# Transposing the last token tiles and the blocks' tokens on TensorE instead of by DMA

## The chip, the cores and the metric

The program runs on one core of a Trainium2 chip. A core has TensorE (PE in the profile; PEld is its weight load), VectorE (DVE), ScalarE (ACT), GpSimd (POOL) and SyncE (SP); SP and POOL issue the transfers here, SP ordinary ones and DMA transposes, POOL the ones that gather or scatter rows by a table of row numbers. Each engine works through its own instructions in the order in which they were emitted and waits on semaphores for the others. The metric is the device time in microseconds of one execution.

## The reference

Three layers follow one another on 1536 tokens of 512 numbers:

```
x = attention(q, k, v)            # only pairs whose 6 hash bits agree; 2 x 8 heads of 768 x 64
out = sum over e of P[:, e] * (relu(x @ w1[e]) @ w2[e])     # first mixture: 8 experts, 1024 hidden units
idx = argmax(normalised(x) @ normalised(emb).T / tau)       # second mixture: each token goes to one expert
out[mask_e] = gate * (relu(x[mask_e] @ w1b[e]) @ w2b[e])    # mask_e: the tokens with idx == e
```

The kernel keeps numbers as two float16 parts, a high and a low one, and forms a product from three matmuls (high x high, high x low, low x high).

## The kernel before

**Up to the last expert.** Attention, and the first mixture with each expert's first product in Winograd's form, fill the first 1167 us or so. They are not touched.

**The last products of the first mixture.** The tokens are twelve tiles of 128, numbered 0 to 11 in the order in which they are finished. Tiles 8 to 11 come last, in `mm2s(E - 1, 2, last_tile)` (line 1569): 24 matmuls of 512 columns for each tile (line 932). When a tile's sum is complete, `finish_tile` (line 1059) adds it to `acc` on VectorE (L1425), writes its high part on ScalarE (L195) and its low part on VectorE (L196) into rows `xf`, has SP transpose these rows into `xt` by DMA (L1067), and has SP write the rows to memory (L1069) for later gathers.

**The router.** For each tile `route_logits` (12 tiny matmuls, L1078, tile `rl`, which read `xt`; then five small VectorE steps, L1081 to L1085) picks the tokens' experts, and `route_rank` (two tiny matmuls, L1089 and L1090, then VectorE) counts each token's place within its expert. After tile 11 `place` sorts the remaining tokens into blocks of at most 128 tokens of one expert: a long chain of small VectorE steps (L1138 to L1108), 12 tiny matmuls (`pid`, L1171), then the blocks' row numbers (L1175), the six first gathers of tokens, and the gates (L1022 to L1317 on VectorE, then 24 tiny matmuls `pg`, L1323).

**The blocks of the second mixture.** 22 slots are laid out, of which four can be filled from the first eight tiles alone, before the last tiles are known; in the profiled execution 17 blocks ran (0 to 16). A block j takes its tokens' rows by a gather on POOL (`gather_x`, L1362), which SP transposes by DMA (L1364), and its weights by two gathers on POOL (`gather_w`, L1345), unless they are there already. `block1(j)` is 96 matmuls of 128 columns (L1381) in two halves, each followed by ScalarE (L1386) and VectorE (L1387); `block2(j)` is 24 matmuls of 512 columns (L1398), then VectorE scales (L1407) and POOL scatters the result (L1412).

**What sets the order.** From line 1515 on an agenda does: `paced(gen, per)` counts a step after every `per` matmuls it emits, and `at(d, f)` puts `f` d steps later. A step is 4 matmuls in the last products (six steps for a tile), 32 in `block1` and 8 in `block2` (six steps for a block). `DT = (20, 15, 10, 6)` steps after tiles 8, 9, 10 and 11 come their logits, `DR` steps after that the rank. Since TensorE works in emission order, a tiny matmul that waits for a transfer holds all matmuls behind it.

Of the kernel before, what the change touches and what calls it, by code (L numbers as in the profile page):

```python
# [10 lines left out]
F16 = mybir.dt.float16  # L11
# [22 lines left out]
# columns of the constant table: they follow from the shapes alone  # L34
# [56 lines left out]
class Plan:  # L91
    """Puts tasks in the order in which the engines would come to them: each engine takes the task of lowest
    rank whose inputs are there and whose buffers are free. Tasks are then emitted in that order."""
# [58 lines left out]
def tile_kernel(ctx, tc, q, k, v, proj, wg, w1, w2, emb, tau, w1b, w2b, cst, out):  # L152
# [76 lines left out]
    def plan_pair(p):  # L229
# [6 lines left out]
        # load  # L236
# [11 lines left out]
        def qk(w):  # L248
# [28 lines left out]
            if not first:  # L277
                a = add(("hi", p, w), he, hu, hi(slice(0, 2)), after=[L[w]], rank=rk, take=take)
                a = add(("lo", p, w), DVE, 0.98, lo(slice(0, 2)), after=[a], rank=rk)
            else:  # L280
                # the first head waits for nothing else: its way to the tensor engine is the shortest
                h0 = add(("hi0", w), ACT, 0.4, hi(0), after=[L[w]], rank=-90, take=take, order=[T.get(("hi0", 0))])
                l0 = add(("lo0", w), DVE, 0.46, lo(0), after=[h0], rank=-90)
                t0 = add(("pt", w), PE, 0.65, tr0, after=[l0, T["ident"]], rank=-90, take=("st",))
                cb = add(("cb", w), ACT, 0.75, lambda: nc.scalar.activation(out=Bt[i][:, 0], in_=q_.t[w], func=AF.Copy), after=[t0], rank=-85)
                add(("ca", w), DVE, 0.87, lambda: nc.vector.tensor_copy(out=At[i][0:64, 0], in_=q_.t[w][r:r + 64]), after=[t0], order=[cb], rank=-85, give=("st",))

                def bits0(m):
                    q_.__dict__.setdefault("pb", {})[w] = mx_tile(m)
                    for g in range(2):  # L290
                        for n in range(3):
                            nc.tensor.matmul(out=q_.pb[w][64:96, g, 0:384], lhsT=Wp[w][n], rhs=Bt[i][:, 0, g * 384:(g + 1) * 384], start=(n == 0), stop=(n == 2))

                def thr0():
                    s1, s2 = (cc["thr"], cc["msc"]) if w == 0 else (cc["thrk"], cc["msck"])
                    nc.vector.tensor_scalar(out=At[i][64:88, 0].rearrange("p (g s) -> p g s", g=2), in0=q_.pb[w][64:88, :, 0:384],
                                            scalar1=s1[64:88], scalar2=s2[64:88], op0=ALU.is_gt, op1=ALU.mult)

                bd = add(("bd", w), PE, 1.5, bits0, after=[cb, T["pj2"]], rank=-84, take=(MX,))
                add(("bt", w), DVE, 0.87, thr0, after=[bd], rank=-84, give=(bd,))  # L300
                a = add(("hi", p, w), ACT, 0.4, hi(1), after=[L[w]], order=[h0, T.get(("hi0", 0))], rank=-80)
                a = add(("lo", p, w), DVE, 0.46, lo(1), after=[a], rank=-80)
# [14 lines left out]
        # bits of the hash  # L317
# [26 lines left out]
        # sums of the values  # L344
# [19 lines left out]
        # the pair's columns of x, in two parts, transposed  # L364
# [23 lines left out]
    def plan_head(p, a, q_, C, V, SV):  # L388
# [44 lines left out]
        # the first head's halves follow one another; the others have their maxima in time  # L433
# [11 lines left out]
        for g in range(2):  # L445
# [3 lines left out]
            for c0 in range(0, NC, 2):  # L449
# [17 lines left out]
                def l(eng, g_=g_, c0=c0):  # L467
                    # the upper halves of float32 are bfloat16 values: the first part; the second is what they leave
# [44 lines left out]
    def w_piece(dst, src, j, m):  # L513
        """rows j*m*128.. of src [rows, n] into dst[:, j*m:(j+1)*m, 2, n]"""
        n = src.shape[1]
        t = sgp.tile([P, m, n], F32, tag="sg", name="sg")
        nc.sync.dma_start(out=t, in_=src[j * m * P:(j + 1) * m * P].rearrange("(c p) f -> p c f", p=P))
        return t
# [26 lines left out]
    def mm1(pool, ps_tile, e, t0, n):  # L545
        """hidden units of tokens t0..t0+n"""
# [22 lines left out]
    with tc.manual_schedule():  # L569
# [19 lines left out]
        def pj_parts():  # L589
            # the projection in three parts whose products with the parts of q and k are exact  # L590
# [35 lines left out]
        # the accumulators of the filling products take the place of one of the tiles for the maximum  # L626
# [9 lines left out]
        def fill():  # L636
            """the first expert on the first half of the tokens, in pieces that fill the tensor engine's pauses"""
# [91 lines left out]
        # the parts of the tokens' sums (see mm1s), and the weights' parts: five pieces that take turns  # L729
# [5 lines left out]
        # scratch: the second mixture's weights in two parts, a row for each expert and partition  # L735
# [42 lines left out]
        def w1_jobs(e, p):  # L778
            """columns p and p + 4 of W1 (in chunks of 128), quarters a11 and a12 above a21 and a22 (columns by rows),
            and the sums of quarters; parts of a11, a12, a22, s2, s3, s4, s1"""  # L780
# [32 lines left out]
        # every split is preceded by its load, sgp_bufs pieces ahead  # L813
# [23 lines left out]
        def unit_x(k, l, u, h):  # L837
            """a half of a unit's tokens: a half's tokens meet tokens of the same sequence in the other half"""
# [4 lines left out]
        def token_sums(u):  # L843
            """B12 - B11 (T1), B22 - B12 (T3), B21 - T2 (T4) and B22 - T1 (T2) of the quarters B of x (halves of its
            columns by halves of the unit's tokens)"""
# [26 lines left out]
        def mm1s(e, u):  # L872
            """hidden units of a unit, two tiles in each half: of the quarters of W1 and x, seven products instead
            of eight (Winograd's form of Strassen's algorithm)"""
# [144 lines left out]
        def newton_sqrt(n, p, out, sq, tmp):  # L1019
            """out = sqrt(sq), the table's value refined once"""  # L1020
# [38 lines left out]
        def finish_tile(o):  # L1059
            """a token tile's mixture is complete: keep it in two parts, and choose its expert"""  # L1060
# [6 lines left out]
            nc.sync.dma_start_transpose(out=xt, in_=xf)  # L1067
# [4 lines left out]
            return xt  # L1072
# [25 lines left out]
        def rank_parts(t0, t1):  # L1098
            """the full blocks before each rank and its place in its block"""
# [35 lines left out]
        def count_blocks(limits, op):  # L1135
            """how many of the limits each expert's tokens reach; the sums up to each expert"""
# [4 lines left out]
        def order_blocks():  # L1141
            """experts with more blocks come first; the blocks before each expert's and up to them"""
# [7 lines left out]
        def slot_experts(j0, j1, blocks):  # L1150
            """the expert of each slot's block; expert 0 without a block"""
# [21 lines left out]
        def slot_reads(ps, j0, j1):  # L1173
            """an empty place reads row 0 and writes nowhere"""
# [7 lines left out]
        def early_place():  # L1182
            """The first tiles hold at least one full block of an expert's tokens, whatever the choices: the first
            such blocks are the first slots. A slot that gets none stays empty."""
# [19 lines left out]
        def early_rest_of_loads():  # L1204
            """what needs the space of the last products' operands"""
# [42 lines left out]
        def place():  # L1248
            """the other blocks, of at most 128 tokens of one expert"""
# [10 lines left out]
            # a third of the blocks for each weight buffer, its blocks in that order  # L1260
# [7 lines left out]
        def late_experts(jb, ld):  # L1268
            """a slot's weights are fetched unless their buffer holds them already"""
# [60 lines left out]
        BW = {}  # L1330
        xbT = {}
# [23 lines left out]
        def gather_x(j):  # L1355
# [8 lines left out]
            turn = lambda: nc.sync.dma_start_transpose(out=xbT[j], in_=xb)  # L1364
            if j == 3:
                at(X3T, turn)
            else:
                turn()
# [40 lines left out]
        def scatter(n):  # L1409
            """the first of the outputs that are ready go to their rows"""  # L1410
# [21 lines left out]
        def route_step():  # L1432
            """moves the tiles that are complete through the router, a stage at a time"""
# [10 lines left out]
        def run(gen, per, jobs=None, n=1):  # L1444
            """emits a unit's matmuls; after every `per` of them a piece of other engines' work, `jobs` in `n` pieces"""
# [11 lines left out]
        def start_expert(e):  # L1457
            """the work beside this expert's products: the next expert's weights, the second mixture's weights"""
# [3 lines left out]
            def spread(heavy, light, n=1, m=0):  # L1462
                """the second half of a piece comes after n light ones"""
# [67 lines left out]
        def last_tile(t, ps):  # L1531
            mix(E - 1)(t, ps)
            at(DT[t - TE], route_logits, t, pending.pop()[1])
# [42 lines left out]
        at(W3T, third_weights)  # L1576
        for j in range(2):
            paced(block1(j), 32)
            paced(block2(j), 8)
# [5 lines left out]
        # each slot that may stay empty has its condition; the last ones, which hardly any choice of experts needs, share one  # L1585
        c = ExitStack()
        for j in range(2, NBLK):
# [7 lines left out]
            if EARLY < j and j + XAHEAD - 1 < NBLK:  # L1595
                gather_x(j + XAHEAD - 1)
            paced(block2(j), 8)
# [7 lines left out]
DT = (20, 15, 10, 6)  # L1605
DR = (2, 2, 2, 2)
# [12 lines left out]
X3T = 12  # L1619
# [37 lines left out]
```

## Time and profile before

| | us |
|---|---|
| median of 3 runs | 1446.8 |
| lowest and highest | 1440.62, 1452.34 |
| profiled execution, first to last instruction (span) | 1424.0 |
| TensorE busy, in the profiled execution | 1338.6 (94%) |
| VectorE, ScalarE, GpSimd busy | 842.0, 529.7, 507.2 |

Of the profiled execution only the span is given; it is 22.8 us under the median of the three runs, which also hold what lies around the instructions. The stretch that the change touches is the last sixth, from about 1167 us on. Times in a row are from the span's start. A bracket at a row's end is the idle time of its engine just ahead of it, and what ended it; "issue" means that nothing in the trace held the engine.

### The profile page before, as it was taken

To read this page: it belongs to the slowest core of one execution; us is meant where nothing else is said; L and a number is where in the kernel's file an instruction comes from. 1 tells how busy PE (TensorE), PEld (TensorE's weight loads), DVE (VectorE), ACT (ScalarE), POOL (GpSimd) and SP (SyncE) were. 2 spreads that over 40 slices of the span, in tenths; PEclk is the share of its full clock that TensorE was granted. 3 is DMA by queue.
4 is the path that set the end of the run, shared out by engine and by line. 5 is a ranking of instruction groups with operands and counts; after the bars stand their busy time and mean duration, and the time that the engine had idled before them with its cause. 6 is when DMAs were issued, how large, how long until landed. Compare 5 with 4: busy or idle time off the path is not lost.

```text
span 1424.0 us, 28018 instructions
## 1 busy us (share of the span) xinstructions
PE 1338.6 (94%) x11536; PEld 888.9 (62%) x11536; DVE 842.0 (59%) x1590; ACT 529.7 (37%) x799; POOL 507.2 (36%) x406
## 2 busy tenths in 40 slices
PE   5888999989999999999999999999999997699996
PEld 3565666545666666666666666666666664466664
DVE  8999764158576765765775676576665573421111
ACT  3576544233444444434443443343343331001110
POOL 4667746042465421431431342142141122123321
PEclk9999999999999999999999999999999999899998
DMA  5664401212145426434332443643511249498595
GB/s 156 155 193 124 102 18 13 56 60 105 45 134 177 133 74 207 134 104 154 99 111 103 135 127 104 207 134 104 193 44 45 68 137 299 143 315 306 187 320 139
DMA packets 152813, 194.61 MB, mean 137 GB/s; under 512 B 79246, under 2 KB 114910, under 8 KB 149864
## 3 DMA queue, kind: packets, MB, share of 16 engines
q1 hardware_dynamic: 146392, 137.70, 33.1%
q0 software_dynamic: 6288, 55.06, 10.9%
q8 instruction: 93, 1.52, 0.4%
q14 instruction: 40, 0.33, 0.1%
HBM read 128.76 MB, written 43.25 MB: 121 GB/s over the span
## 4 chain that ended last, share of the span: by engine, by line
PE 75%; DVE 11%; DMA 4%; issue 3%; POOL 3%; SPq 2%; ACT 1%; another core or an unknown queue 0%; DVEq 0%; POOLq 0%; ACTq 0%
PE h L932 28%; PE h L887 25%; PE h L1381 4%; PE y L1398 4%; DVE m L404 3%; PE st L457 2%; DMA w1m<-W1S,widx 2%; PE av L479 2%; PE hy L688 2%; PE hy L658 2%; PE h L552 1%; PE h L564 1%; POOL tc L853 1%; DMA tq<-tq 1%; SPq L1364 1%
## 5 line engine op out<-in xcount | busy, mean ns | idle before, releaser
L932 PE MATMUL h<-w,ht 128*128 128x512 f16 x2016 | 439.6, 379 | 0.0
L932 PEld LDWEIGHTS <-ht 128*128 128x128 f16 x2016 | 196.4, 98 | 231.8 <-POOL ht L903 0.3
L903 POOL TENSOR_TENSOR ht<-C,ht 128x1024 f16<-128x1024 f32 x63 | 134.2, 2130 | 522.9 <-ACT C L902 520.3
L894 DVE TENSOR_TENSOR C<-h,C 128x256 f32<-128x256 f32 x588 | 230.6, 420 | 129.4 <-PE h L887 118.2
L887 PEld LDWEIGHTS <-wm 128*128 128x128 f16 x2268 | 221.4, 98 | 31.7 <-issue 3.7
L472 POOL TENSOR_TENSOR el<-e 128x768 f16<-128x768 f32 x85 | 132.8, 1568 | 87.0 <-ACT e L460 86.4
L887 PE MATMUL h<-Tq,wm 128*128 128x256 f16 x1296 | 159.5, 273 | 0.9 <-DVE Tq L862 0.9
L887 PEld LDWEIGHTS <-wx 128*128 128x128 f16 x1260 | 122.9, 98 | 15.7
L887 PE MATMUL h<-xT,wm 128*128 128x256 f16 x972 | 127.7, 273 | 2.2 <-DVE acc L1425 1.1
L917 ACT ACTIVATE C<-h 128x256 f32<-128x256 f32 x84 | 32.1, 382 | 232.1 <-PE h L887 139.7
L196 DVE SCALAR_TENSOR_TENSOR pre<-sg,pre 128x1024 f16<-128x1024 f32 x64 | 86.3, 1356 | 51.6 <-ACT pre L195 51.6
L460 ACT ACTIVATE e<-st 128x384 f32<-128x384 f32 x192 | 86.5, 489 | 64.5 <-PE st L457 61.3
L898 ACT ACTIVATE ht<-C 128x1024 f16<-128x1024 f32 x84 | 88.3, 1051 | 39.8 <-DVE C L894 39.7
L195 ACT ACTIVATE pre<-sg 128x1024 f16<-128x1024 f32 x64 | 66.7, 1051 | 93.6 <-DMA W1S<-pre 33.7
L1398 PE MATMUL y<-bw,hx 128*128 128x512 f16 x408 | 96.5, 393 | 0.3 <-ACT hx L1386 0.2
L1425 DVE SCALAR_TENSOR_TENSOR acc<-h,Pm,acc 128x512 f32<-128x512 f32 x84 | 62.6, 745 | 53.2 <-PE h L932 52.5
L1386 ACT ACTIVATE hx<-h 128x512 f16<-128x512 f32 x34 | 20.3, 597 | 186.0 <-PE h L1381 122.3
L887 PE MATMUL h<-Tq,wx 128*128 128x256 f16 x720 | 88.7, 273 | 0.0
L804 POOL TENSOR_TENSOR tq<-sw 128x256 f32<-128x256 f32 x56 | 52.3, 935 | 74.7 <-PE hy L688 31.1
L1387 DVE SCALAR_TENSOR_TENSOR hx<-h,hx 128x512 f16<-128x512 f32 x34 | 23.5, 691 | 89.4 <-ACT hx L1386 82.7
L479 PEld LDWEIGHTS <-e 128*128 128x128 bf16 x1152 | 64.1, 98 | 13.1 <-issue 1.9
L887 PE MATMUL h<-xT,wx 128*128 128x256 f16 x540 | 72.2, 273 | 0.0
(300 smaller groups left out, 1982.0 us busy)
## 6 DMA issues: line engine op xcount, KB each, us to landing
sg<-in_moe_w_dram SPq DMA_DIRECT2D x100, 512.0 KB
W1S<-pre SPq DMA_DIRECT2D x32, 512.0 KB
W2S<-pre SPq DMA_DIRECT2D x32, 512.0 KB
sw<-in_moe_w_dram SPq DMA_DIRECT2D x56, 256.0 KB
ld<-in_q_dram SPq DMA_DIRECT2D x8, 384.0 KB
ld<-in_k_dram SPq DMA_DIRECT2D x8, 384.0 KB
ld<-in_v_dram SPq DMA_DIRECT2D x8, 384.0 KB
X2D<-xx SPq DMA_DIRECT2D x8, 256.0 KB
```

What stands on the lines that cost most here:

```text
L195: nc.scalar.activation(out=hi, in_=src, func=AF.Copy, scale=scale)
L196: nc.vector.scalar_tensor_tensor(out=lo, in0=src, scalar=scale, in1=hi, op0=ALU.mult, op1=ALU.subtract)
L460: nc.scalar.activation(out=g_.e[c0][:, c % 2, :], in_=g_.st.pop(c), func=AF.Exp, scale=2.0 ** -11)
L472: (nc.gpsimd if eng == POOL else nc.vector).tensor_tensor(out=g_.el[c0], in0=e, in1=hi, op=ALU.subtract)
L479: mm = lambda out, l, r, start=False, stop=False: nc.tensor.matmul(out=out, lhsT=l, rhs=r, start=start, stop=stop, skip_group_check=True)
L887: nc.tensor.matmul(out=ps[:, 0:UT], lhsT=w[:, i, c * P:(c + 1) * P], rhs=b(kc, j), start=(m == 0), stop=(m == len(seq) - 1))
L894: nc.vector.tensor_tensor(out=o, in0=ps[:, 0:UT], in1=x, op=ALU.add)
L898: nc.scalar.activation(out=hi, in_=C, func=AF.Relu)
L903: nc.gpsimd.tensor_tensor(out=lo, in0=C, in1=hi, op=ALU.subtract)
L932: nc.tensor.matmul(out=ps, lhsT=ht[:, a, p, h, i * P:(i + 1) * P], rhs=W2[e][:, h * 4 + p, b, :], start=(m == 0), stop=(m == len(seq) - 1))
L1398: nc.tensor.matmul(out=y, lhsT=h[:, fc, a, :], rhs=w[:, fc, b, :], start=(m == 0), stop=(m == len(seq) - 1))
L1425: nc.vector.scalar_tensor_tensor(out=acc[:, t, :], in0=ps, scalar=Pm[:, t, e:e + 1], in1=acc[:, t, :], op0=ALU.mult, op1=ALU.add)
```

## The change

- The DMA transposes of tiles 8 to 11 and of all blocks' rows go (tiles 0 to 7 keep theirs).
- A new function `turn` does each on TensorE: eight transposes of 128 x 128 into a PSUM tile `tn`, and one VectorE copy of 128 x 1024 to `xt`.
- Tiles 8 to 11 are turned `TT` = 4, 4, 4, 2 steps after they are finished; their logits come after `DT` = 7, 7, 6, 3 steps in place of 20, 15, 10, 6, their ranks after 2, 2, 1, 1 more in place of 2, 2, 2, 2. So `place` comes four steps earlier in the emission order.
- Block 0's rows are turned just ahead of its first product, those of block j + 1 between the two products of block j.

```diff
         split(xf[:, 0:DM], xf[:, DM:], acc[:, t, :], 512.0)
         nc.scalar.activation(out=jk, in_=acc[:, t, :], func=AF.Square, accum_out=ss[:, o, :])
-            nc.sync.dma_start_transpose(out=xt, in_=xf)
+            if o < TE:
+                nc.sync.dma_start_transpose(out=xt, in_=xf)
...
-            return xt
+            return xt if o < TE else (xt, xf)
+
+        def turn(xt, xf):
+            ps = ps_.h.tile([P, 2 * KC, P], F16, tag="h", name="tn")
+            for c in range(2 * KC):
+                nc.tensor.transpose(out=ps[:, c, :], in_=xf[:, c * P:(c + 1) * P], identity=ident)
+            nc.vector.tensor_copy(out=xt, in_=ps)
...
-            turn = lambda: nc.sync.dma_start_transpose(out=xbT[j], in_=xb)
-            if j == 3:
-                at(X3T, turn)
+            if j < TURN:
+                xrow[j] = xb
             else:
-                turn()
+                nc.sync.dma_start_transpose(out=xbT[j], in_=xb)
+
+        def turn_x(j):
+            if j < min(TURN, NBLK):
+                turn(xbT[j], xrow.pop(j))
...
             mix(E - 1)(t, ps)
-            at(DT[t - TE], route_logits, t, pending.pop()[1])
+            xt, xf = pending.pop()[1]
+            at(TT[t - TE], turn, xt, xf)
+            at(DT[t - TE], route_logits, t, xt)
             at(DT[t - TE] + DR[t - TE], ranked, t)
...
+        turn_x(0)
         for j in range(2):
             paced(block1(j), 32)
+            turn_x(j + 1)
             paced(block2(j), 8)
...
             paced(block1(j), 32)
             if EARLY < j and j + XAHEAD - 1 < NBLK:
                 gather_x(j + XAHEAD - 1)
+            turn_x(j + 1)
             paced(block2(j), 8)
...
-DT = (20, 15, 10, 6)
-DR = (2, 2, 2, 2)
+TURN = 99
+TT = (4, 4, 4, 2)
+DT = (7, 7, 6, 3)
+DR = (2, 2, 1, 1)
```

The first place is SP's queue at the last tiles, before the change: tiles 9 and 10 (`xT`, `tq`) stand behind the rows of blocks 0 to 2 (`xs`), and tile 11 behind those of block 3.

```order
L1364 DMA_TRANSPOSE xs<-xs 128x8x128 x3
L1067 DMA_TRANSPOSE xT<-xT 128x8x128
L1069 DMA X2D<-xT 128x1024
L1067 DMA_TRANSPOSE tq_14144<-tq_14144 128x8x128
L1069 DMA X2D<-tq_14144 128x1024
L1364 DMA_TRANSPOSE xs<-xs 128x8x128
```

The same place after the change; `xx` is a tile of 0 to 7.

```order
L1068 DMA_TRANSPOSE xx<-xx 128x8x128
L1070 DMA X2D<-xx 128x1024
L1072 DMA X2E<-xx 128x1024
L1070 DMA X2D<-xT 128x1024 x2
L1070 DMA X2D<-tq_14144 128x1024 x2
```

SP issues only the writes of the last tiles' rows, and nothing for the blocks.

The second place is VectorE around the end of the last products, before the change: the sum and the low part of tile 11, then a half of block 0's first product, then tile 8's logits.

```order
L1425 SCALAR_TENSOR_TENSOR acc<-h,Pm,acc 128x512
L196 SCALAR_TENSOR_TENSOR tq_14144<-acc,tq_14144 128x512
L1387 SCALAR_TENSOR_TENSOR hx<-h,hx 128x4x128
L1081 TENSOR_SCALAR L<-rl,invtau 128x8
L1082 TENSOR_REDUCE M<-L 128x1
```

The same place after the change: the logits of tile 10, the sum and low part of tile 11, the copy of block 0's turned rows.

```order
L1089 TENSOR_SCALAR L<-rl,invtau 128x8
L1090 TENSOR_REDUCE M<-L 128x1
L1091 SCALAR_TENSOR_TENSOR w<-L,M,cf 128x8
L1092 TENSOR_REDUCE mw<-w 128x1
L1093 TENSOR_SCALAR OH<-cf,mw 128x8
L1436 SCALAR_TENSOR_TENSOR acc<-h,Pm,acc 128x512
L196 SCALAR_TENSOR_TENSOR tq_14144<-acc,tq_14144 128x512
L1080 COPY xs<-tn 128x1024
```

Three tiles' logits are done by then, and the copy, which block 0's first matmul needs, is the last of eight steps.

## Rows read from the trace of the kernel before

**Rows 1.** The page's first line.
```profile
span 1424.0 us, 28018 instructions
```

**Rows 2.** Timeline of PE: start us, us, engine, line, op, count, [idle before <-releaser].
```profile
1176.71 13.11 PE L932 MATMUL h<-w,ht 128*128 128x512 f16 x60
1189.66 3.74 PE L1381 MATMUL h<-xs,xT 128*128 128x128 f16 x64
...
1200.98 0.48 PE L1078 MATMUL rl<-enT,xT 128*128 128x8 f16 x12 [5.49 <-DMA xT<-xT]
1201.32 3.24 PE L1398 MATMUL y<-bw,hx 128*128 128x512 f16 x8
...
1207.10 0.46 PE L1078 MATMUL rl<-enT,tq 128*128 128x8 f16 x12 [2.51 <-DMA tq<-tq]
1207.41 3.52 PE L1398 MATMUL y<-bw,hx 128*128 128x512 f16 x8
...
1220.90 0.48 PE L1078 MATMUL rl<-enT,tq 128*128 128x8 f16 x12 [8.13 <-DMA tq<-tq]
1221.24 5.30 PE L1381 MATMUL h<-xs,xT 128*128 128x128 f16 x64
...
1233.40 1.95 PE L1381 MATMUL h<-xs,tq 128*128 128x128 f16 x32
...
1240.92 0.45 PE L1323 MATMUL pg<-BI,A 128*128 128x22 f16 x12 [0.91 <-DVE gl L1315]
...
1247.76 0.18 PE L1323 MATMUL pg<-BI,A 128*128 128x22 f16 x1 [1.35 <-issue]
1247.78 7.41 PE L1398 MATMUL y<-bw,hx 128*128 128x512 f16 x24
1255.03 5.52 PE L1381 MATMUL h<-xs,w1m 128*128 128x128 f16 x96
1260.39 5.34 PE L1398 MATMUL y<-bw,hx 128*128 128x512 f16 x24
```

**Rows 3.** Chain that ended last: start us, us, what.
```profile
1206.09 14.76 DMA tq<-tq
```

**Rows 4.** Stretches: us, busy PE, PEld, DVE, ACT, POOL, PEclk, DMA share, GB/s.
```profile
1203.50:1221.00 17.50, 6.86 (x41) 2.98 (x40) 2.26 (x17) 0.00 (x0) 1.98 (x2) 0.79 1.05 328
1245.30:1265.50 20.20, 18.02 (x149) 10.79 (x149) 4.32 (x7) 1.79 (x3) 3.02 (x3) 0.84 1.10 286
```

**Rows 5.** Lines 273 and 286, attention's first head: duration ns min/median/max, first and last start.
```profile
L273 PE MATMUL st<-ident,nat x12: 262/311/312, 11.7 to 12.8; 128*128 128x128 f16 x12
L286 DVE COPY QA<-st x1: 560/560/560, 13.4 to 13.4; 64x768 f16<-64x768 f16 x1
```

**Rows 6.** Timeline of DVE, from tile 8's sum to the gates.
```profile
1176.34 0.74 DVE L1425 SCALAR_TENSOR_TENSOR acc<-h,Pm,acc 128x512 f32<-128x512 f32 x1
1177.77 0.69 DVE L196 SCALAR_TENSOR_TENSOR xT<-acc,xT 128x512 f16<-128x512 f32 x1 [0.69 <-ACT xT L195]
...
1193.84 0.22 DVE L1081 TENSOR_SCALAR L<-rl,invtau 128x8 f32<-128x8 f32 x1
...
1194.75 0.23 DVE L1085 TENSOR_SCALAR OH<-cf,mw 128x8 f16<-128x8 f32 x1
...
1227.40 0.26 DVE L1138 TENSOR_TENSOR t<-base,cf 128x96 f32<-128x96 f32 x1
...
1235.32 0.87 DVE L1108 TENSOR_SCALAR A<-cf,rank 128x128 f16<-128x128 f32 x4
1236.46 0.18 DVE L1175 TENSOR_SCALAR idx<-pid 128x18 int32<-128x18 f32 x1 [0.28 <-PE pid L1171]
...
1240.79 0.43 DVE L1317 TENSOR_TENSOR BI<-Bk,gl 128x264 f16<-128x264 f32 x1
```

**Rows 7.** Waits from 1200 us on: who waited, total us, times, longest.
```profile
PE h L1381 <- issue: 6.3, 15, 1.3
```

**Rows 8.** Timeline of POOL: block 4's first weights.
```profile
1245.33 1.00 POOL L1345 DMA_INDIRECT xT<-W1S,widx  x1 [0.30 <-issue]
```

More of the change, by code (lines that the diff above doesn't have):

```diff
@@ L1330, in tile_kernel @@
         BW = {}
-        xbT = {}
+        xbT, xrow = {}, {}
         hb = {}
@@ L1618 @@
 PM1 = 7
-X3T = 12
 EP = (13, 2, 5)
```

## Prediction

> **What bounds the kernel now.** The page's first line gives the span, 1424.0 us [rows 1]. The runs' median, 1446.8 us, lies 22.8 above it, and I take that difference as unchanged: the sum below is made on the profiled execution and its result is subtracted from the median.
>
> I read TensorE's timeline first. To the end of the last products at 1189.66 TensorE has no hole that this change touches: 60 matmuls of 512 columns in 12.95 us, 0.216 us each [rows 2]. The end is just as dense: block 3 starts at 1255.03 and its two products follow at full pace, 96 matmuls in 5.36 us (0.056 us each), and 24 in 5.18 us at 0.216. A block is 10.54 us of matmuls. In between, however, blocks 0, 1 and 2 take from 1189.66 to 1255.03, that is 65.4 us for 31.6 us of their own matmuls [rows 2]. The reader should see three things there.
>
> First, three waits of logits for a DMA transpose: 5.49, 2.51 and 8.13 us, together 16.1 us, with all matmuls of blocks 0 and 1 queued behind them [rows 2]. The last transpose took 14.76 us to land [rows 3], with the DMA engines fully busy [rows 4].
>
> Second, the clock. After the waits, 8 matmuls that need 1.73 us took 3.24 and 3.52 us, 64 that need 3.57 took some 5.1 (5.30 with the tail of the last), and 24 that need 5.18 took 7.25 [rows 2]; the granted clock averaged 0.79 and 0.84 in these stretches [rows 4]. [...] They cost about 1.5, 1.8, 1.6 and 2.1, together 7 us.
>
> Third, the 24 tiny matmuls of the gates: 12 of them took 0.45 us, but from 1240.92 to the last at 1247.76 it is 6.8 us, with holes up to 1.35 us whose cause is "issue", so no semaphore [rows 2]. Warm and fed they would be 0.9 us: 5.9 us lost.
>
> **What the change removes.** All three waits, since SP's transposes are no longer on the way, and the tail of the router comes four steps earlier. What remains is to walk TensorE through the new order from 1176.71 to the start of block 3.
>
> **Prices.** One turn is eight pairs of weight load and 128-column matmul. The nearest row is `block1`, the same shape with a weight load for each matmul: 8 x 0.056 = 0.45 us. Upper bound: the kernel's own transposes at its start, 12 in 12.8 + 0.31 - 11.7 = 1.4 us, 0.12 each [rows 5], so 0.94 us a turn; I take 0.45, since those ran at the cold start. The copy of 128 x 1024: 768 columns took 0.56 us [rows 5], hence 0.75 us at most by proportion; I take 0.70. A sum, high and low part of a tile: 1176.34 to 1178.46, 2.12 us; the five logit steps: 1193.84 to 1194.98, 1.14 us [rows 6]. A tile's logits on TensorE: 0.34 us from 1200.98 to the next matmul [rows 2].
>
> [...]
>
> **The last products.** Tiles 8, 9 and 10 add three turns (1.35 us) and three logits (1.02). Tile 8's turn comes 4 matmuls after 1176.71, at 1177.6, but its low part is ready at 1178.46 [rows 6]; four transposes of the high part go first, so 0.7 us of wait. The ranks of tiles 8 and 9 come 12 matmuls and the logits after the next tile's end (2.6 + 0.34 = 2.9 us), while VectorE first does that tile's sum and low part and then the logits (2.12 + 1.14 = 3.3): 0.45 us of wait each. Sum 4.0: the last products and tile 10's logits end at 1193.6.
>
> **A new wait ahead of block 0.** Its first matmul needs the copied rows, and the copy stands on VectorE behind tile 10's logits and tile 11's sum and low part, none of which can be earlier: 1.14 + 2.12 + 0.70 and 0.2 for hand-overs, 4.2 us. Behind it waits everything. Block 0 starts at 1197.8, where before it started with no wait. The rows after the waits of 2.51 and 5.49 us ran at the lower clock, so I add 1.7 us.
>
> **Blocks 0 to 2.** Block 0: 10.54, two turns 0.9, logits of tile 11 0.34, clock 1.7: to 1211.3. Tile 11's rank falls at about 1207.8, and from there VectorE's chain of `place`, 1227.40 to 1236.19 less one half of a block (0.7) [rows 6], is 8.1 us: done at 1216.3. Block 1's first product ends at 1216.7, so this chain, which ran beside matmuls before too, is just covered. Row numbers' matmuls 1.1, turn 0.45, 16 matmuls 3.45: TensorE reaches the gates at 1221.7. VectorE needs 4.76 us from the row numbers to the last gate (1236.46 to 1241.22) [rows 6] and starts at 1218.0: 1.1 us of wait to 1222.8. The gates' matmuls 0.9, the other 8 matmuls 1.7: block 2 starts at 1225.4, where it was 1233.40, and holds no gates any more. Block 2: 10.54 + 0.45, and 1.3 for a hole of the kind "issue", the longest that a `block1` shows [rows 7], since block 4's weight gather now falls into it. Block 3 starts at 1237.7 instead of 1255.03: 17.3 us gained.
>
> **Given back.** Blocks 3 to 16 each carry one turn of the next rows: 14 x 0.45 = 6.3 us. Their copies hide: 0.70 us on VectorE under 5.18 us of `block2`, with two halves (0.69 each) ahead of it; if VectorE ran 3 us late the next block would wait. POOL's queue keeps its order; a gather now waits for TensorE's turn, a block old. SP issues nothing in the blocks. The rest of the kernel is the same.
>
> Sum: -17.3 + 6.3 = -11.0 us, span 1413.0, time 1446.8 - 11 = 1436 us (0.8% less).
>
> Bounds of what I could not read: the clock after the new wait 0 to 3.4 us (none, or twice); the turn up to 0.94 instead of 0.45, 21 x 0.49 = 10.3 us; holes in block 2 from 0 to the 5.9 us that the gates had.
>
> **Rivals.**
>
> *A. The holes go too.* If the DMA transposes are what delays the supply of instructions, block 2's 1.3 us and the 6.3 us in 15 holes of later blocks [rows 7] vanish: -18.6, time 1428. For it: the worst holes, in the gates, came with six row gathers and the transposes in the queue and the DMA share at 1.10 [rows 4]. Against it: the weight gathers alone keep the queues full, and they stay. [...] The rows name no cause but "issue". Chance 0.2.
>
> *B. A turn costs nearer to its upper bound*, or the new order waits more on VectorE than I found: half of the way to 0.94 is 5 us, all of it 10: -6 to -1, time 1441 to 1446, as good as no change, and the work has only changed its waiter. For it: transposes read one operand from an identity and write 16-bit numbers, which no warm row shows. Chance 0.12.
>
> *C. Weights late, slower than before.* Block 4's weights were issued at 1245.33 [rows 8] for a block that started at 1265.57, 20.2 us later, without a wait. In the new order they are issued in block 2, at 1229, for 1248.7: 19.7 us. The gathers for blocks 2 and 3 come nearer to them too, since they are emitted behind tile 11. If the weights then need more than 19.7 us, TensorE waits; once they need more than 19.7 + 11.0 = 30.7, the kernel is slower than before; at 36 us it is 5 us slower, 1452, with the clock 1.7 more. Against it: the queue moved 286 GB/s there with transposes in it [rows 4], a pair is 4.2 MB (128 rows of two times 16 KB), 15 us at that rate, and the transposes leave. Chance 0.05.
>
> *D. Transposes do not overlap.* At 311 ns each [rows 5] a turn is 2.5 us, 21 turns give 43 us more than forecast: 1479. The 12 transposes in 1.4 us speak against it. Chance 0.03.
>
> **The numbers.** The forecast, -16 to -6 us, has the rest, 0.60. A measurement of this kernel can tell about 1%, 14.5 us, from no change. Faster by over 1% (under 1432.3) is most of A and a tail of the forecast: 0.26. Slower by over 1% is D and a part of C: 0.05. Within 1%: 0.69. The range 1427 to 1446 takes in A, the forecast and B; outside are C, D and the far ends.
>
> **What would show it.** Right, if in the new profile no `rl` waits for a DMA; TensorE stands idle about 4 us ahead of block 0, ended by VectorE's copy; a turn takes 0.45 us from its first transpose to the next matmul; the gates' matmuls take about 1 us; block 3 starts near 1238; later blocks follow at some 11.0 us instead of 10.5. Wrong, if `block1` waits for a weight gather (C), turns last over 0.9 us (B, D), or the holes of the kind "issue" change by several us either way (A).

## The result, and the profile after

| | us |
|---|---|
| before, the runs shown ahead of the prediction and one more | median 1449.6 (1440.6 to 1476.4, 4 runs) |
| after | median 1405.0 (1404.6 to 1407.3, 4 runs) |
| ratio | 0.973, 95% interval 0.968 to 0.978 |
| predicted | 1436 (1427 to 1446), on 1446.8 |

The change gained 41.8 us on the 1446.8 that the prediction started from, nearly four times what it forecast, and the time lies 22 us below its range. Ratios here and below compare, for each kernel, only its runs within 1.5% of its fastest; the kernel before loses many of its slower runs by that (21 of 35 in the first group below), so a ratio is nearer to 1 than that of the medians.

The profiled execution after took 1404.6 us; its page's first line, and of the queues those of SP (q1) and POOL (q0):

```profile
span 1402.6 us, 28323 instructions
...
q1 hardware_dynamic: 118936, 130.88, 30.7%
q0 software_dynamic: 6288, 55.06, 10.3%
```

Before, q1 had 146392 packets of 137.70 MB: the 26 transposes, of 1056 packets of some 250 bytes each, are gone.

The run took 2.0 us more than its span. The 22.8 us between the span of before [rows 1] and its median can't be what lies around the instructions. This is the first thing that the prediction had wrong, and the experiments turn on it.

TensorE's timeline after, from tile 10's logits on; columns as in [rows 2]:

```profile
1194.15 0.45 PE L1086 MATMUL rl<-enT,tq 128*128 128x8 f16 x12
1194.45 0.61 PE L1079 MATMUL tn<-ident,xs 128*128 128x128 f16 x8
1198.48 3.36 PE L1392 MATMUL h<-xs,xT 128*128 128x128 f16 x32 [3.41 <-DVE xs L1080]
...
1223.40 0.79 PE L1331 MATMUL pg<-BI,A 128*128 128x22 f16 x24 [1.40 <-DVE BI L1324]
...
1225.77 5.52 PE L1392 MATMUL h<-xs,tq 128*128 128x128 f16 x96
1231.13 0.61 PE L1079 MATMUL tn<-ident,xs 128*128 128x128 f16 x8
1231.58 5.34 PE L1409 MATMUL y<-bw,hx 128*128 128x512 f16 x24
1236.76 5.52 PE L1392 MATMUL h<-xs,w1m 128*128 128x128 f16 x96
1242.12 0.61 PE L1079 MATMUL tn<-ident,hx 128*128 128x128 f16 x8
1242.57 5.34 PE L1409 MATMUL y<-bw,hx 128*128 128x512 f16 x24
```

Block 0 waits 3.41 us for VectorE's copy of its rows, its first 32 matmuls take 3.2 us to the next row instead of 1.8 (the granted clock averaged 0.54 there), the 24 matmuls of the gates run without a hole, block 3 starts at 1236.76, and a turn takes 1242.57 - 1242.12 = 0.45 us. All that TensorE waits for from 1150 us on (who, released by whom, us in total, times, longest):

```profile
PE h L1392 <- DVE xs L1080: 3.4, 1, 3.4
PE pg L1331 <- DVE BI L1324: 1.4, 1, 1.4
PE h L887 <- DVE C L894: 1.1, 1, 1.1
PE rk L1097 <- DVE OH L1093: 1.1, 3, 0.4
PE tn L1079 <- DVE xT L196: 0.3, 1, 0.3
```

No row for a DMA is left, and none of the kind "issue": [rows 7] has no successor.

### The profile page after: what moved, and what is told of

Read it like the earlier page. It is cut to its first block, busy times and chain, and to the rows that moved or that the text cites. A ratio compares the mean times of both kernels' runs of the same rounds, so it can differ in the third digit from the quotient of the medians.

```text
span 1402.6 us, 28323 instructions
## 1 busy us (share of the span) xinstructions
PE 1340.4 (96%) x11712; PEld 896.4 (64%) x11712; DVE 857.3 (61%) x1612; ACT 529.6 (38%) x799; POOL 507.4 (36%) x406
## 4 chain that ended last, share of the span: by engine, by line
PE 77%; DVE 12%; DMA 4%; POOL 3%; issue 3%; ACT 2%; SPq 0%; POOLq 0%; DVEq 0%
PE h L932 29%; PE h L887 25%; PE h L1392 5%; PE y L1409 4%; DVE m L404 3%; PE st L457 2%; DMA w1m<-W1S,widx 2%; PE av L479 2%; PE hy L688 2%; PE hy L658 2%; PE h L552 1%; PE h L564 1%; POOL tc L853 1%; PE mx L400 1%; DMA tq<-W1S,widx 1%
## 5 line engine op out<-in xcount | busy, mean ns | idle before, releaser
L887 PEld LDWEIGHTS <-wm 128*128 128x128 f16 x2268 | 221.3, 98 | 31.9 <-issue 3.7
L1409 PE MATMUL y<-bw,hx 128*128 128x512 f16 x408 | 91.2, 379 | 0.0
L479 PE MATMUL av<-vh,el 128*128 128x65 f16 x576 | 66.2, 193 | 4.2 <-DVE el L472 3.8
```

The lines of the kernel that those rows point to most:

```text
L479: mm = lambda out, l, r, start=False, stop=False: nc.tensor.matmul(out=out, lhsT=l, rhs=r, start=start, stop=stop, skip_group_check=True)
L887: nc.tensor.matmul(out=ps[:, 0:UT], lhsT=w[:, i, c * P:(c + 1) * P], rhs=b(kc, j), start=(m == 0), stop=(m == len(seq) - 1))
L1409: nc.tensor.matmul(out=y, lhsT=h[:, fc, a, :], rhs=w[:, fc, b, :], start=(m == 0), stop=(m == len(seq) - 1))
```

## Experiments

Two theories stood at the start. **H, late data**: DMA transposes make other transfers late, by an amount that differs from run to run, and the usual run of before has much of that while its profiled run had little. **W, waits of the logits**: the three waits of [rows 2] are nearly all of it. A third put the 22.8 us outside the span. The runs went to four chips in groups of four, four, four and three (e1 to e4, e5 to e8, e9 to e12, e13 to e15), and one finding is that chips differ, so times are compared within a group. Medians of the kernel before in the groups: 1442.8 (35 runs), 1446.7, 1450.2 and 1445.0 (11 runs each).

### The kernels themselves again

**e1**, the kernel before, no edit. Expected: 

> The kernel before, unchanged, for the span of every timed run. Theory H (holes): time minus span is about 2 us as in the changed kernel, and the span itself is 1438 or more in most runs, so the profiled execution of 1424.0 was a lucky one; the holes in TensorE's matmuls are longer than its 6.3 us. Theory O (outside): spans stay near 1424 and time minus span is about 20 us. Ratio 1.00 either way.

Measured: 1446.8 (1416.0 to 1473.5, 13 runs). The profiled execution took 1459.5 with a span of 1457.6, so nothing of note lies outside the span. Its TensorE timeline late in the blocks, and the queues in 1390 to 1400 us (queue, packets, MB, time of the packets as a share of 16 engines):

```profile
1388.14 5.34 PE L1398 MATMUL y<-bw,hx 128*128 128x512 f16 x24
1422.78 7.63 PE L1381 MATMUL h<-tq,w1m 128*128 128x128 f16 x96 [29.30 <-DMA w1m<-W1S,widx]
```
```profile
DMA packets 368, 0.99 MB, mean 99 GB/s; under 512 B 306, under 2 KB 306, under 8 KB 314
...
q1 hardware_dynamic: 297, 0.07, 76.0%
q0 software_dynamic: 71, 0.92, 30.8%
```

A block waited 29.3 us for its weights. Meanwhile a DMA transpose was in flight: 297 of its packets held 76% of the engines' time, 0.76 x 160 / 297 = 0.41 us each, and the queues together moved 99 GB/s. That is what H expects, as far as the weights go.

**e13**, the same on the last chip. Expected: 

> The kernel before unchanged, profiled beside the changed kernel on one chip. Theory of the late weights: waits of a block for its weights of 10 to 40 us in all in the profile, beside some 16 us of logits' waits; holes of the kind issue only if the changed kernel beside it has them too (0, or 10 to 13 us in both). Theory that DMA transposes make the holes: 10 us or more of holes here, none in the changed kernel beside it. Median 1440 to 1450 by both.

Measured: 1438.9 (1423.1 to 1446.9), profiled span 1445.1. Its waits:

```profile
PE h L1381 <- DMA xT<-W1S,widx: 15.6, 1, 15.6
PE rl L1078 <- DMA xT<-xT: 10.4, 1, 10.4
PE h L1381 <- issue: 8.7, 15, 1.2
PE pg L1323 <- issue: 6.5, 9, 1.2
PE h L1381 <- DMA w1m<-W1S,widx: 3.1, 1, 3.1
```

In e1 it was block 15 that waited long; here it is block 4 (15.6 us), and block 15 waits only 3.1. As expected of late weights, 18.7 us in two waits.

**e5, e9 and e14**, the changed kernel, no edit, on the second, third and fourth chip. Expected: 

> The changed kernel unchanged, as a base for the three beside it, and to see whether the absence of holes of the kind issue in its blocks belongs to the kernel or to one execution. Belongs to the kernel: 1404 to 1408 us in nearly all runs, the blocks from 3 on 10.99 us each in the profile, no hole of the kind issue over 0.3 us in them. Belongs to the execution: runs spread over some 1404 to 1417, the profile with 5 to 11 us of such holes, and the holes of the runs with transposes say nothing on the transposes.

 

> The changed kernel unchanged, as the base of the three beside it on this chip. It has given 1405.0 once, with no hole of the kind issue in its blocks, and 1418.3 on another chip, with 11 us of them. If the holes go with the chip: one of these two values again, all runs within 4 us of each other. If they go with the execution: a mixture of both.

 

> The changed kernel unchanged, beside the kernel before. If the holes belong to the chip: 1405 with none, or 1418 with 11 us of them, and the same kind in the kernel before. If they belong to the transposes: 1405 without holes.

Measured: 1418.3 (1416.9 to 1420.0), 1405.4 (1403.4 to 1407.1) and 1419.4 (1415.6 to 1421.6), ratios to before beside them 0.986 (0.981 to 0.990), 0.973 (0.967 to 0.979) and 0.991 (0.986 to 0.996). Narrow on each chip, in two values 13 us apart. Block 2 of e5, and then of e9:

```profile
1225.99 1.11 PE L1392 MATMUL h<-xs,tq 128*128 128x128 f16 x17
...
1230.23 2.05 PE L1392 MATMUL h<-xs,tq 128*128 128x128 f16 x33 [1.03 <-issue]
...
1235.32 0.61 PE L1079 MATMUL tn<-ident,xs 128*128 128x128 f16 x8
```
```profile
1228.61 5.52 PE L1392 MATMUL h<-xs,tq 128*128 128x128 f16 x96
1233.97 0.61 PE L1079 MATMUL tn<-ident,xs 128*128 128x128 f16 x8
```

From the block's first matmul to its turn it is 9.33 us in e5 and 5.36 in e9, 4.0 us more: 2.9 us in six holes of the kind "issue", of which the longest is shown, and matmuls drawn out between them. With those of blocks 4, 6, 7, 10 and 11 e5 has 19 holes, 8.8 us of idle time. On the fourth chip both kernels have them (8.7 us of `h` in e13 as in e14). So the holes go with the chip (or its session, for each chip had only one), not with the transposes: H, whose expectations said that transposes make them, falls in this part.

### Halves of the change

**e2**, `TURN = 0`: only the tiles are turned on TensorE, the blocks' rows by DMA. Expected: 

> Tiles 8 to 11 are turned on TensorE as in the change, all blocks' rows by DMA as before. Theory H (the DMA transposes of the blocks make TensorE's holes, of different length in each run): 1418 to 1432 us with a wide spread, holes with the releaser issue in the blocks. Theory W (the waits of the last tiles' logits are nearly all of the gain, and longer than profiled in a usual run of before): 1398 to 1410 us, below or level with the change, since 18 turns of 0.45 us are saved.

Measured: 1434.3 (1422.1 to 1464.7), on e1's chip; ratio 1.003 (0.999 to 1.007). The spread of before is still there, and so is a wait for late weights in the profile (8.4 us). The waits of the logits for a DMA are gone, and the median falls by only 8.5 us: W falls.

**e3 and e10**: only the blocks' rows are turned on TensorE, the tiles by DMA.

```diff
-            if o < TE:
-                nc.sync.dma_start_transpose(out=xt, in_=xf)
+            nc.sync.dma_start_transpose(out=xt, in_=xf)
...
-DT = (7, 7, 6, 3)
+DT = (20, 15, 10, 6)
```

Expected: 

> All blocks' rows are turned on TensorE, tiles 8 to 11 by DMA with their old steps. Theory H: no holes in the blocks, but some waits of the logits are left: 1408 to 1425 us with a narrow spread. Theory W: the waits stay and the turns come on top: 1435 to 1455 us.

 

> Only the blocks' rows are transposed on TensorE, the last four tiles by DMA in the old order (1417.9 in its first run, with holes, on another chip than the changed kernel's runs). If the tiles' part of the change is worth 13 us on its own, as a comparison across the chips had it: 13 slower than the changed kernel beside it. If that difference was the holes' alone: within 4 us of it, since without the blocks' transposes no logits waited for a transpose.

Measured: e3 1417.9 (1416.4 to 1420.1, 12 runs) where before had 1442.8, ratio 0.992 (0.990 to 0.994); e10 1400.9 (1399.2 to 1401.7) where the whole change had 1405.4. The spread is gone with the blocks' transposes alone, and so are the waits of the logits for tiles that are still transposed by DMA. All of e10's waits from 1150 us on:

```profile
PE h L1391 <- DVE xs L1079: 2.4, 1, 2.4
PE h L887 <- DVE C L894: 1.1, 1, 1.1
PE pg L1330 <- DVE BI L1323: 0.9, 1, 0.9
PE rk L1096 <- DVE OH L1092: 0.3, 1, 0.3
PE pid L1178 <- DVE BI L1291: 0.3, 1, 0.3
```

There is no row for `rl`. In before, the tiles' transposes stand on SP's queue behind those of the first blocks' rows, which stand beside gathers of weights. e13's queue of SP there (start us, us):

```profile
1185.19 13.18 SPq L1364 DMA_TRANSPOSE xs<-xs  x3
1198.46 1.26 SPq L1067 DMA_TRANSPOSE xT<-xT  x1
```

Three transposes of blocks' rows take 13.18 us, and tile 9's starts only then; its logits come at 1207.65, 9.2 us behind that start, so it is slow to land as well. With the blocks' transposes away the tiles' land in time. The blocks' part is thus the whole gain. The tiles' part, beside it, costs 4.5 us (e9 and e10, on one chip): four turns of 0.45 make 1.8, and the waits listed for after come to 7.3 us, for e10 to 5.0.

### What a DMA transpose does to the other transfers

**e4, e6 and e7**: the changed kernel with an unused transfer behind each gather of a block's rows: a transpose, a plain copy in rows of 2 KB, a plain copy in 1024 pieces of 256 bytes.

```diff
                 xrow[j] = xb
+                idle = m2_.p.tile([P, 2 * KC, P], F16, tag="idle", name="idle")
+                nc.sync.dma_start_transpose(out=idle, in_=xb)                        # e4
+                nc.sync.dma_start(out=idle, in_=xb.rearrange("p (c s) -> p c s", s=P))   # e6; e7 into a padded tile
```

Expected: 

> The changed kernel, and every gathered block of rows is also transposed by DMA into a tile that nobody reads (22 slots; no wait of TensorE on them). Theory H: holes with the releaser issue come back in the blocks, 10 to 30 us slower than the change (1415 to 1435), with a wide spread. Theory W and any theory in which only waits on the transposes' results count: within 3 us of the change (1402 to 1408).

 

> The changed kernel, and behind each gather of a block's rows an unused plain copy of these rows (128 rows of 2 KB) on SP's queue, in place of the unused transpose of the run before; nothing reads it. If the transposition itself is what slows the weights' gathers and brings the holes (median 1426.7 with it): 1404 to 1410 us, no wait for weights. If 256 KB more in the queues for each block are enough: 1420 to 1430, with waits for weights of 5 us or more and holes of the kind issue as with the transposes.

 

> As the run with unused plain copies, but written in pieces of 256 bytes, 1024 of them for a block, about as many packets as a transpose makes. If the count of small packets is what the weights' gathers suffer from: 1415 to 1430 us, with waits for weights. If it is what the transposition does within the queue: 1404 to 1411.

Measured: e4 1426.7 (1419.0 to 1452.6, 12 runs); e6 1420.4 (1418.3 to 1421.3) and e7 1420.4 (1418.4 to 1422.3), both 2 us over e5 beside them. e4 has no run of the changed kernel on its chip; it is 8.8 us over e3 there, and its spread is 34 us, where e3, e6 and e7 spread over 3 to 4. Its profiled execution, the slowest of the twelve, waits for weights again, twice:

```profile
PE h L1394 <- DMA w1m<-W1S,widx: 17.6, 1, 17.6
...
PE h L1394 <- DMA tq<-W1S,widx: 8.3, 1, 8.3
```

The plain copies move the same bytes, e7's in 1024 pieces where a transpose makes 1056 packets, and with two of them beside the gathers the queues still move 332 GB/s in e6 and 301 in e7 (1225 to 1240 us). So neither the bytes nor the number of small packets does it, but the transposition. e4's holes, which H expected of the transposes, are those of a chip: e3 has them there without any block's transpose.

**e12**: slots 0 to 9 by DMA, from slot 10 on by TensorE.

```diff
-            if j < TURN:
+            if j >= LATE:                # LATE = 10
```

Expected: 

> The changed kernel with the blocks' rows up to slot 9 transposed by DMA again, and only those from slot 10 on by TensorE. With all blocks by DMA it was 1434.3, spread over 1422 to 1465. If the spread comes from transposes in the queues together with the weights' gathers of the late blocks: runs within 6 us of each other, 0 to 6 over the base, no wait of a block from 9 on for its weights. If the early ones do it as well: spread of 20 us or more and a median 10 over the base.

Measured: 1408.2, but spread over 1397.2 to 1415.2; neither value of the expectation. One early collision is enough. Its profiled execution has one wait for a DMA, block 4's, and on SP's queue two transposes issued over 36.5 us (of the tiles' four in e10, the first three take 1.24 to 1.32 each):

```profile
1259.11 7.27 PE L1392 MATMUL h<-hx,xT 128*128 128x128 f16 x96 [15.72 <-DMA xT<-W1S,widx]
```
```profile
1225.57 36.54 SPq L1375 DMA_TRANSPOSE xT<-xT  x2
```

The queues of e12, and then of e9, both in 1229 to 1239 us on the same chip:

```profile
DMA packets 657, 0.78 MB, mean 78 GB/s; under 512 B 618, under 2 KB 618, under 8 KB 619
...
q0 software_dynamic: 42, 0.63, 127.2%
q1 hardware_dynamic: 615, 0.16, 86.3%
```
```profile
DMA packets 391, 3.05 MB, mean 305 GB/s; under 512 B 64, under 2 KB 64, under 8 KB 252
...
q0 software_dynamic: 391, 3.05, 86.1%
```

With transposes and the weights' gather in flight together the queues move a quarter as much, and a packet of POOL's queue takes 1.272 x 160 / 42 = 4.8 us instead of 0.35 (0.861 x 160 / 391; packets of 15 and 7.8 KB on average). The weights, issued at 1224.19, are late by 15.7 us. It is not that the engines are full: in the next 10 us of e12, 1239 to 1249, the packets fill 36% of the engines' time, and the queues move less still:

```profile
DMA packets 195, 0.66 MB, mean 66 GB/s; under 512 B 152, under 2 KB 152, under 8 KB 159
...
q0 software_dynamic: 48, 0.62, 22.5%
q1 hardware_dynamic: 147, 0.04, 13.8%
```

Nor does every meeting slow the weights: in 1360 to 1380 us of e1 two transposes are under way for 31.9 us beside gathers of weights, and the queues move 366 to 388 GB/s. What decides between the two stays open.

The two quickest runs of e12, 1397.2 and 1398.4, beat the changed kernel (1405.4). They were not profiled; the profiled span, 1413.5, less the wait of 15.7 is 1397.8, so they are probably runs without a collision. Ten turns fewer stand on TensorE's path then (4.5 us), and ahead of block 0 no copy is waited for. On SP's queue in e10 a transpose of 256 KB takes 1.24 us and the plain write of the same rows behind it 0.57, so a transpose takes longer there too; beside gathered weights the rows above differ far more, and they decide.

### Versions that could beat both

**e8**: block 0's turn moves ahead of tile 10's logits. **e11**: that, and five of the six gathers ahead of block 2 follow later, four steps apart. **e15**: e8's edit on e3's kernel.

```diff
+            if t == NTILE - 2:
+                at(5, turn_x, 0)         # e8, e11, e15; turn_x(0) ahead of block 0 goes
...
-            for j in range(EARLY, EARLY + XAHEAD):
-                gather_x(j)
+            gather_x(EARLY)              # e11
+            for j in range(1, XAHEAD):
+                at(4 * j, gather_x, EARLY + j)
```

Expected: 

> The changed kernel with the first block's turn moved ahead: its eight transposes are issued 20 matmuls after the end of tile 10's products, five steps of four, so that VectorE copies them ahead of tile 11's sum. The first block's matmuls then follow tile 10's logits at once. If the wait of 3.4 us and the spell at the lower clock behind it (1.5) were on the path: 1400 us (1399 to 1402), block 0 starting near 1194.5, no wait of h for xs. If they only covered VectorE's chain of the last tile: 1404 to 1406, with about 3 to 5 us of waits appearing at the row numbers or the gates instead.

 

> The kernel with the earlier first turn, and of the six gathers of rows that POOL issues one behind the other ahead of block 2 only the first stays there; the others follow four steps (some 7 us) apart. If POOL's issue of gathers one after another makes the holes: block 2's holes, 4 us where the base has any, fall below 1 us, and the time is 3 us under the early turn alone, so 7 under the base (1411, or 1401 beside a base of 1405). If the holes do not depend on it: 4 under the base, block 2's holes as long as before, perhaps moved.

 

> The blocks' part alone (1400.9 beside 1405.4 of the whole change), with the first block's turn issued 20 matmuls after tile 10's products as in the run with the early turn, which took 3.6 off the whole change. If the wait of 2.4 us ahead of block 0 and its spell at the lower clock are on the path here too: 3 to 4 us under the blocks' part alone, that is 8 under the changed kernel beside it. If VectorE's chain of the last tile then sets the start of block 2: 5 under it, with the difference as waits of the row numbers or the gates.

Measured: e8 1414.7 (1412.1 to 1415.2), 3.6 under e5. On a base of 1405 the expectation asked for 3 to 6 under it. The timeline shows why: block 0 follows at once and at full pace (32 matmuls in 1.95 us, where e5's first 32 take 3.32).

```profile
1192.92 0.61 PE L1079 MATMUL tn<-ident,xs 128*128 128x128 f16 x8
1193.37 1.03 PE L932 MATMUL h<-w,ht 128*128 128x512 f16 x4
1194.23 0.45 PE L1086 MATMUL rl<-enT,tq 128*128 128x8 f16 x12
1194.53 1.95 PE L1392 MATMUL h<-xs,xT 128*128 128x128 f16 x32
```

e11 1400.2 (1398.8 to 1401.5), 5.2 under e9; but that chip has no holes, so what the spreading would do to holes was not told, and e8's edit did not run alone there, so neither was what the spreading is worth. e15 went wrong: 1431.3 (1418.4 to 1450.9), 12 over e14 where 8 under it was expected. Its profiled execution:

```profile
PE rl L1085 <- DMA tq<-tq: 16.5, 2, 15.5
```

Starting block 0 earlier let POOL issue block 1's and 2's weights from 3.4 us behind the start of the last tile's transpose on (1195.65 and 1192.24) rather than from 8.0 on (1202.43 and 1194.48 in e10), and tile 11's logits waited 15.5 us for it. Meanwhile, in 1204 to 1218 us, the queues move 107 GB/s. The tiles' transposes, too, seem to collide when weights come close to them. Of the versions measured, e11 is the best without any DMA transpose in this stretch; e10 is as fast (1400.9) but keeps four.

## Why the prediction was wrong

- **The step that failed is the first: "I take that difference as unchanged."** The profiled execution of before was one of its quick ones, and the 22.8 us that the usual run takes longer are, all but some 2, time within the span, which the change removes. After, median and span differ by 2.4 us, so 20.4 of the gain come from there. What is in it, e1 and e13 show: their spans are 33.6 and 21.1 us longer than that of [rows 1], and in them blocks wait 29.3 and 18.7 us for weights, which no block does in the profiled execution of before. The median of a kernel whose runs spread over 57 us (e1; the three that the prediction had, over 12) was treated as a constant on top of one run.
- **Rival C looked at late weights in one direction only.** It priced them for the new order from one quick execution, where block 4's weights needed less than 20.2 us [rows 8], and noted that "the transposes leave" as a mere point against it. That e4 brings the waits back with unused transposes and e6 and e7 don't says that their leaving was the main effect of the change.
- **Rival A's holes went, but not for its reason.** It priced them at 7.6 us; none is left in the trace after, and between the two spans that is worth 9.4 us beyond the walk (below): 6.3 us of idle time [rows 7] and matmuls drawn out between the holes. But on the fourth chip, where both kernels were profiled, e13 and e14 have 8.7 us each in the blocks' first products, and the four profiles on the third chip have none, e12 with its many transposes included. That the trace after has none is thus the luck of its chip. Nor does the program alone make them: the same one, with the same branches, had 8.8 us of holes in e5 and none in e9.
- **The walk was right.** Predicted and found: tile 10's logits end at 1193.6, 1194.45; block 0 starts at 1197.8, 1198.48; block 2 at 1225.4, 1225.77; block 3 at 1237.7, 1236.76; a turn 0.45, 0.45; the copy 0.70, 0.69; a block 11.0, 10.99. Block 3 is 18.3 us earlier than in [rows 2] (17.3 predicted, with 1.3 for a hole in block 2 that did not come), 14 turns give 6.3 back: 12.0 of the 21.4 us between the spans, the rest the holes. Two small slips did no harm: 22 turns run and not 21, since the rows of a slot without a block are turned in the last block, and the slow transposes of [rows 5] ran at a granted clock of 1.00 (11.6 to 13.2 us), so a lower clock at the start is not why they took 0.12 us each.
- **What bounded the old stretch was only half named.** The prediction put the 16.1 us of logits' waits down to SP's transposes as a whole. e3 and e10 have no such wait with the tiles' transposes still on DMA: the blocks' transposes were the cause, and to end the waits the tiles' turns were not needed. The wait ahead of block 0 that the prediction added was real, and avoidable (e8).
- **Rivals B and D** did not happen; the transposes of a turn overlap as [rows 5] let expect: eight take 0.45 us, where a single one lasted 0.31 there.

Of the 41.8 us: 12.0 the walk, 9.4 holes that this execution lacked, 20.4 what the usual run of before has over its quick one, by e1 and e13 mostly late weights. That last share is an estimate, for e1's and e13's profiled executions took 12.7 and 7.9 us longer than the medians of their own runs. On the fourth chip, where both kernels have holes, the medians differ by 25.6 (1445.0 and 1419.4), on the second, where the changed one has them, by 28.4. On the third, where the changed kernel has no holes, they differ by 44.8; whether before has holes there was not profiled. Why some chips show holes stays open. They fall where POOL issues gathers one behind the other (in e5 eight from 1220.20 to 1230.54 us, and block 2's holes from 1227.10 to 1233.41), but in e9 the same eight gathers, from 1222.83 to 1231.95, make none.

## What to carry to other kernels

When the profiled execution is quicker than the median by more than a few us, find out what the slower runs have before building a sum on it: profile the kernel again, and look for a wait that changes its place. Here a DMA transpose in flight together with large gathers was a risk that the one quick trace did not show: no block waited for weights in it, in e1 one waited 29.3 us. Taking the blocks' transposes off the queues was worth more (24.9 us in e3) than ending the waits that the trace showed (8.5 in e2). Of a change with two parts, ask for each whether the other already removes its wait.

## What the runs showed of the hardware

- A DMA transpose and a gather of weights in flight together: 66 to 107 GB/s for 10 us and more at a time (e1, e12, e4 and e15), where gathers alone move 305 in the same stretch as e12's (e9), and with the engines' time filled to 36% (e12) and 26% (e15) only; but also 366 to 388 GB/s (e1). Plain copies of the same bytes beside the gathers cost 2 us over the whole kernel (e6 and e7, 1420.4 on e5's 1418.3).
- Eight transposes on TensorE with their weight loads: 0.45 us (after), as fast as matmuls of that shape (96 of block 3 in 5.36 us, 0.45 for eight); the VectorE copy of 128 x 1024 float16 out of PSUM: 0.68 to 0.69 us.
- The same program shows no holes on TensorE (e9) or 8.8 and 8.7 us of them (e5 and e14, in both in the first products of blocks 2, 4, 6, 7, 10 and 11), from one chip to another, and takes 13 us longer with them (1418.3 and 1419.4 against 1405.4).
